# Agent attention with a gated convolution: queries ahead of the first keys, joined score runs, urgent row copies

## Chip, core and metric

One NeuronCore of a Trainium2 chip runs the whole program. The metric is device time in microseconds of one execution, from the median of three timed runs. The engines are TensorE (PE), VectorE (DVE), ScalarE (ACT), GpSimd (POOL) and SyncE (SP), which issues nearly all transfers.

## What is computed

Four batches of 12,800 positions with 128 channels; 49 agents in each batch.

```python
def sm(a, b):
    s = scale * (a @ b.transpose(0, 2, 1))
    s = s - s.max(-1, keepdims=True)
    e = np.exp(s)
    return e / (e.sum(-1, keepdims=True) + 1e-09)
agent_v = sm(agents, k) @ v
x = sm(q, agents) @ agent_v                     # 4 x 12800 x 128
gate_pre = sum(conv_w[k] * x_shifted_by(4 - k) for k in range(5))   # causal, along positions
gate = 1 / (1 + exp(-gate_pre))
out = (gate * (x @ w_val)) @ w_out
```

(The sum over shifts is written out here in short; the reference pads four zeros in front.)

## The kernel before

Positions of a batch are cut into 10 units of 1,280. Units are counted through all batches (0 to 39); pair p is units 2p and 2p + 1. For the output a batch is cut into 25 chunks of 512 (two and a half chunks a unit), counted 0 to 99, the last of them split in two.

The work is written as a list of steps with short names, `x b.u`:

- `k b.u`: scores of a key unit against the agents (TensorE, 16 products in f32, line 391, into one of two PSUM banks `sc`), copied out by ScalarE (line 417), and the maximum of the unit by VectorE (line 426).
- `m b`, in two steps: the maximum over the ten units, turned and spread by TensorE, VectorE and TensorE again, to the bias of the exponents (`kbias`, line 472).
- `v b.u`: exponents of the keys (ScalarE, line 486), turned in 32x32 blocks by VectorE (line 401), and summed against v on TensorE (line 495).
- `f b`, in five steps: the agents' values of a batch are folded with the convolution and the two weight matrices into ready stationary matrices (`stat`, `wo`). Gates of a batch need it.
- `q b.u`: scores of a query unit (TensorE, into a bank `sc`), turned by VectorE (line 401), maximum (VectorE, line 760), difference (GpSimd, line 765), exponent (ScalarE, line 773), sum and reciprocal (VectorE, lines 778, 779, 782), product (VectorE, line 787), and then a high and a low half in f16 in `pt` (ScalarE line 794, GpSimd lines 800 and 808).
- `t b.u`: `pt` is transposed into `x1`, for units 0 to 3 by TensorE (line 863, copied out by ScalarE and VectorE, lines 870 and 875), for all others by a transposing transfer on SP's queue (line 849). Behind that come the row copies (line 898): some rows of `x1` are copied into `x2`, each shifted by 0 to 4 positions, one pair of transfers for each of units 0 to 3, then one pair of transfers for two units at once.
- `g t`, `a t`, `o t`: gate of a chunk (five products from `x1`, line 937, and one from `x2`, line 941, then tanh on ScalarE), values (lines 964 and 968, then VectorE 977, ScalarE 983, GpSimd 988), and projection (lines 1007 to 1009, ScalarE 1021, store from line 1036).

What sets the order: the long string `order` gives the order of the steps, and so that of TensorE's work. The loads of q, k and v stand in the order of their steps, on eleven tiles `ld`, so that a load may run eleven loads ahead. Everything else (the order on VectorE, ScalarE, GpSimd and on SP's queue) is set by `Plan.order`, which runs through all steps with estimated durations and always takes the ready step with the longest chain behind it; `urge` adds to the length of that chain, and by that also to everything that the step needs. Each engine then works strictly through its own row, and SP issues its transfers in its row, each when what it waits for is done.

Of the kernel before, what the change touches and what calls it, by code (L numbers as in the profile page):

```python
# [49 lines left out]
SINGLE = 4  # L50
# [13 lines left out]
SOON = 10.0  # L64
# [6 lines left out]
class Plan:  # L71
# [11 lines left out]
    def add(self, engine, us, fn, reads=(), writes=(), moved=0.0, key=None, urge=0.0):  # L83
        i = len(self.steps)
        need = set()
        for x in reads:
            need |= self.wrote.get(x, set())
        for x in writes:
            need |= self.wrote.get(x, set()) | self.read.get(x, set())
        for x in reads:  # L90
            self.read.setdefault(x, set()).add(i)
        for x in writes:
            self.wrote[x], self.read[x] = {i}, set()
        self.steps.append((engine, us, fn, need, moved, key))
        self.urge.append(urge)
# [84 lines left out]
def tile_agent_attention_gated_conv(  # L180
# [10 lines left out]
    B, C, N = qT.shape  # L191
    A = 49
    NU = N // UNIT
# [19 lines left out]
    m2 = const.tile([P, 2], F32, name="m2")  # L213
# [610 lines left out]
    def row_keys(s, halves):  # L824


        i = s % NX
        return [(x, i, h) for h in halves for x in ("x1", "x1b")] + [("x1h", i)] * (0 in halves)

    def halo(s, read=()):  # L830
        to = x1s[s % NX][:, PAD - HALO : PAD]
        if s * 2 % NU == 0:
            fn = lambda: nc.gpsimd.memset(to, 0.0)
        else:
            fn = lambda: nc.gpsimd.tensor_copy(
                out=to, in_=x1s[(s - 1) % NX][:, PAD + SEG - HALO : PAD + SEG]
            )
        keys = [(x, (s - 1) % NX, 1) for x in ("x1", "x1b")]
        add("pool", 0.19, fn, list(read) + keys, [("x1h", s % NX)])

    def transposes(b, u):
# [3 lines left out]
        if not on_pe(b, u):  # L845
            dst = unit_rows(g)
            add(
                "dma", 1.4,
                lambda: nc.sync.dma_start_transpose(
                    out=dst.rearrange("p (n i) -> p n i", i=P),  # L850
                    in_=pt.rearrange("p n r -> p (n r)"),
                ),
                [(*p_, n) for n in range(3)], [("x1", g // 2 % NX, g % 2)], 2.4,
            )
            shifts(b, u)
            return
# [4 lines left out]
        def matmuls():  # L861
# [14 lines left out]
            [at], [("x1b", g // 2 % NX, g % 2)],  # L876
        )
        shifts(b, u)

    def shifts(b, u):  # L880

        g = b * NU + u
        if g >= SINGLE and g % 2 == 0:
            return
        n = 1 if g < SINGLE else 2
        u0 = u + 1 - n
        s = g // 2
        x2, x1 = x2s[s % 3], x1s[s % NX]
        o = (g + 1 - n) % 2 * UNIT
        src = row_keys(s, range(0, g % 2 + 1))  # L890
        c = PAD - HALO + o
        for r0, r1, first, every, us in X2CUTS:
            first += A
            rows = x1[first : first + 1 + (r1 - r0 - 1) * every : every, c : c + 1]
            view = [rows.ap[0], (1, TAPS), (1, n * UNIT)]
            add(
                "dma", 0.6,
                lambda r0=r0, r1=r1, rows=rows, view=view: nc.sync.dma_start(
                    out=x2[X2B + r0 * TAPS : X2B + r1 * TAPS, o : o + n * UNIT],
                    in_=bass.AP(rows.tensor, rows.offset, view),  # L900
                ),
                src, [("x2", s % 3, o + i * UNIT, r0) for i in range(n)], us * n,
                urge=SOON if g < SINGLE else 0.0,
            )
        if g % 2 and g < SINGLE:
            halo(g // 2 + 1)
# [165 lines left out]
    for b in range(B):  # L1072
        t0 = b * NCH
        for i in range(NU):
            g = b * NU + i + LEAD
# [17 lines left out]
    for t in range(len(chunks) + 2):  # L1093
# [7 lines left out]

    kinds = {"m": "max", "f": "fold"}
    order = (
# [25 lines left out]
    )  # L1129
    first = [(kinds.get(x[0], x[0]), *map(int, x[1:].split("."))) for x in order.split()]  # L1130
    for w in first:
# [70 lines left out]
```

## Time and profile before

| | us |
|---|---|
| timed runs | 422.53, 423.37, 424.21 (median 423.37) |
| the profiled execution | 419.86 |
| its span, from the first to the last instruction | 417.9 |
| TensorE busy | 399.7 (96%) |
| ScalarE, VectorE, GpSimd busy | 307.2, 295.2, 237.4 |

All rows below come from that one profiled execution, with times counted from the start of its span. Busy time of TensorE is modelled from its instructions; successive products overlap, so the distance of their starts tells more than their durations. An instruction's idle time in brackets is that of its engine ahead of it, with the work that ended it.

### The profile page before, as it was taken

Reading aid. Unit: us, or ns where it says so; the run is one execution under the profiler, and the core shown is the slowest. Engines: PE = TensorE matmul, PEld = TensorE weight load, DVE = VectorE, ACT = ScalarE, POOL = GpSimd, SP = SyncE. Lnnn points to the kernel's source line nnn. Section 1 sums busy time; section 2 is a strip of 40 time slices with the busy share of each in tenths; the row PEclk is TensorE's granted clock in tenths of the full one; section 3 lists DMA queues with packets and bytes.
Section 4 is the critical chain, followed back from the end, with each engine's and each line's share of the span. In section 5 each row is a group of like instructions: output and inputs, shape, how many; then the busy total and the mean of one; then the engine's idle time right before and its main releaser. Section 6 shows DMA issues by size and latency. Waiting matters only on the chain.

```text
span 417.9 us, 10098 instructions
## 1 busy us (share of the span) xinstructions
PE 399.7 (96%) x3907; PEld 195.2 (47%) x3907; DVE 295.2 (71%) x570; ACT 307.2 (74%) x524; POOL 237.4 (57%) x303
## 2 busy tenths in 40 slices
PE   4978999999999999999999999999999999999995
PEld 1357334336555443345555543344555544344443
DVE  5866889976885977677796685777757598666231
ACT  6584468778957677678987486778877577788775
POOL 1002458655677566564476555585366577787643
PEclk9989999999999999999999999999999999999999
DMA  8999999999999999999999999999999977663823
GB/s 323 418 417 413 356 361 353 303 338 319 413 334 281 284 321 373 354 264 348 352 399 288 279 320 380 295 350 276 323 350 347 271 204 224 187 173 145 247 107 126
DMA packets 75131, 127.63 MB, mean 305 GB/s; under 512 B 50466, under 2 KB 50850, under 8 KB 75084
## 3 DMA queue, kind: packets, MB, share of 16 engines
q1 hardware_dynamic: 74940, 126.87, 96.3%
q8 instruction: 30, 0.49, 0.5%
q10 hardware_dynamic: 144, 0.13, 0.1%
q14 instruction: 17, 0.14, 0.1%
HBM read 79.25 MB, written 26.21 MB: 252 GB/s over the span
## 4 chain that ended last, share of the span: by engine, by line
PE 78%; DMA 11%; DVE 6%; ACT 1%; issue 1%; SPq 1%; POOL 0%; POOLq 0%; DVEq 0%
PE gate L937 24%; PE sc L391 17%; PE av L495 8%; DMA ld<-vP 6%; PE val L964 5%; PE out L1007 5%; PE gate L941 5%; PE val L968 5%; PE out L1008 5%; PE out L1009 4%; DMA ld<-kT 2%; DMA x<-pt 2%; DMA x<-x 1%; DVE h L977 1%; DVE sT L401 1%
## 5 line engine op out<-in xcount | busy, mean ns | idle before, releaser
L988 POOL TENSOR_TENSOR hl<-h,hh 128x512 f16<-128x512 f32 (+1 forms) x101 | 116.7, 1156 | 97.1 <-ACT hh L983 96.8
L937 PE MATMUL gate<-x,stat 128*128 128x512 f16 (+1 forms) x500 | 124.2, 378 | 0.4 <-ACT th L950 0.3
L977 DVE SCALAR_TENSOR_TENSOR h<-th,val 128x512 f32<-128x512 f32 x100 | 67.8, 678 | 62.1 <-PE out L1008 28.3
L391 PE MATMUL sc<-ld,ag_sb 128*32 128x320 f32 x1280 | 101.4, 447 | 7.3 <-DMA ld<-kT 6.7
L950 ACT ACTIVATE th<-gate,unscale 128x512 f32<-128x512 f32 x100 | 68.3, 683 | 32.7 <-PE gate L941 31.3
L1021 ACT ACTIVATE ob<-out,oscale 128x512 f32<-128x512 f32 x98 | 67.2, 686 | 19.1 <-PE out L1009 16.5
L937 PEld LDWEIGHTS <-stat 128*128 128x128 f16 x505 | 46.1, 97 | 63.3 <-issue 13.1
L983 ACT CAST hh<-h 128x512 f16<-128x512 f32 (+1 forms) x101 | 61.4, 608 | 16.6 <-DVE h L977 16.1
L765 POOL TENSOR_TENSOR qw<-sT,qmx 128x490 f32<-128x490 f32 x40 | 41.3, 1034 | 45.0 <-DVE qmx L760 44.7
L391 PEld LDWEIGHTS sc<-ld,ag_sb 128*32 128x32 f32 x1280 | 36.8, 111 | 58.7 <-issue 25.6
L495 PE MATMUL av<-ld,eT 128*32 128x129 f32 (+1 forms) x1400 | 49.6, 276 | 1.5 <-DVE eT L401 1.2
L495 PEld LDWEIGHTS av<-ld,eT 128*32 128x32 f32 (+1 forms) x1400 | 45.6, 115 | 8.4 <-issue 3.0
L808 POOL TENSOR_TENSOR pt<-qw,pt 128x490 f16<-128x490 f32 x40 | 44.8, 1119 | 1.6 <-ACT pt L794 1.4
L401 DVE STREAM_TRANSPOSE sT<-sc 128x640 f32<-128x640 f32 x40 | 33.5, 837 | 12.9 <-PE sc L391 12.2
L486 ACT ACTIVATE e<-ks,kbias 128x320 f32<-128x320 f32 x80 | 39.2, 553 | 3.5 <-DVE eT L401 2.2
L800 POOL TENSOR_SCALAR pt<-qw 128x240 f16<-128x240 f32 x80 | 27.8, 367 | 22.0 <-DVE qw L787 22.0
L401 DVE STREAM_TRANSPOSE eT<-e 128x640 f32<-128x640 f32 x40 | 33.3, 839 | 9.5 <-ACT e L486 5.3
L941 PE MATMUL gate<-x,stat 128*128 128x512 f16 x100 | 37.8, 378 | 0.5 <-DMA x<-x 0.5
L964 PE MATMUL val<-x,stat 128*128 128x512 f16 x100 | 37.9, 379 | 0.2 <-DVE wo L743 0.2
L968 PE MATMUL val<-x,stat 128*128 128x512 f16 x100 | 37.8, 378 | 0.0
L417 ACT COPY ks<-sc 128x640 f32<-128x640 f32 x40 | 27.6, 690 | 13.4 <-PE sc L391 13.0
L1007 PE MATMUL out<-hh,wo 128*128 128x512 f16 x98 | 37.2, 380 | 0.1
(133 smaller groups left out, 418.9 us busy)
## 6 DMA issues: line engine op xcount, KB each, us to landing
ld<-kT SPq DMA_DIRECT2D x40, 640.0 KB
ld<-qT SPq DMA_DIRECT2D x40, 640.0 KB
ld<-vP SPq DMA_DIRECT2D x39, 645.0 KB
outT<-ob SPq DMA_DIRECT2D x48, 512.0 KB
x<-x SPq DMA_DIRECT2D x18, 300.0 KB
x<-x SPq DMA_DIRECT2D x18, 175.0 KB
outT<-ob SPq DMA_DIRECT2D x3, 256.0 KB
ld<-vP SPq DMA_DIRECT2D x2, 322.5 KB
```

Of the source, the lines that this page charges most:

```text
L391: nc.tensor.matmul(out=out[g * BLK : (g + 1) * BLK, j, 0:GT], lhsT=ag_sb[:, b, j * BLK : (j + 1) * BLK], rhs=src[:, g * GT : (g + 1) * GT] ...
L401: nc.vector.transpose(out=out.rearrange("p n (j i) -> p j n i", j=2), in_=in_.rearrange("p j (n i) -> p j n i", i=BLK),)
L495: nc.tensor.matmul(out=av[o + j : o + j + cols, 0 : C + 1], lhsT=et[:, n, j : j + cols], rhs=vt[:, n, :], start=(u == 0 and n < 2), stop=( ...
L937: nc.tensor.matmul(out=pg, lhsT=stat[:, k, :], rhs=x1[:, c : c + w], start=(k == 0), stop=False,)
L941: nc.tensor.matmul(out=pg, lhsT=stat[:, TAPS + 1, :], rhs=x2[:, o2 : o2 + w], start=False, stop=True,)
L950: lambda: nc.scalar.activation(out=th, in_=pg, func=AF.Tanh, scale=unscale[:, 0:1]),
L964: nc.tensor.matmul(out=pv, lhsT=stat[:, TAPS, :], rhs=x1s[(b * NCH + n0 // CH) // 5 % NX][:, PAD + o2 : PAD + o2 + w], start=True, stop=False,
L968: nc.tensor.matmul(out=pv, lhsT=stat[:, TAPS + 2, :], rhs=x2[:, o2 : o2 + w], start=False, stop=True,)
L977: lambda: nc.vector.scalar_tensor_tensor(out=h, in0=th, scalar=1.0, in1=pv, op0=ALU.add, op1=ALU.mult),
L983: "act", 0.16 + 0.42 * scale, lambda: nc.scalar.copy(out=hh, in_=h),
L988: lambda: nc.gpsimd.tensor_tensor(out=hl, in0=h, in1=hh, op=ALU.subtract),
L1021: lambda: nc.scalar.activation(out=ob[:, o : o + w], in_=po, func=AF.Copy, scale=oscale),
```

## The change

Three edits. The steps q0.0, q0.1 and q0.2 stand ahead of the ten key units of batch 0 instead of behind them, with their transposes t0.0, t0.1 and t0.2 among the keys and the key maximum. In the later part of the order runs of score and sum steps that were parted by a gate, values or projection step are put next to each other, at thirteen places. And `urge` for row copies, which was given for units 0 to 3 (`SINGLE` is 4), is given for units 4 and 5 too, and for the last pair of units of batches 0, 1 and 2.

```diff
-                urge=SOON if g < SINGLE else 0.0,
+                urge=SOON if g < SINGLE + 2 or u == NU - 1 and b < B - 1 else 0.0,
...
-        "k0.0 k0.1 k0.2 k0.3 k0.4 k0.5 k0.6 k0.7 k0.8 k0.9 m0 m0 q0.0 v0.0 v0.1 v0.2 v0.3 v0.4 "
-        "v0.5 v0.6 v0.7 v0.8 v0.9 f0 t0.0 f0 q0.1 k1.0 f0 k1.1 f0 q0.2 g0 k1.2 f0 t0.1 a0 q0.3 "
+        "q0.0 q0.1 q0.2 k0.0 k0.1 k0.2 t0.0 k0.3 k0.4 k0.5 k0.6 k0.7 k0.8 k0.9 t0.1 m0 t0.2 m0 "
+        "v0.0 v0.1 v0.2 v0.3 v0.4 v0.5 v0.6 v0.7 v0.8 v0.9 f0 k1.0 f0 k1.1 k1.2 f0 q0.3 f0 g0 "
...
```

What this makes of the engines' rows at three places (numbers behind names are those of the buffers; `x8` stands for eight equal products, two passes each).

VectorE in the opening, before: from the middle of the weights' unpacking (`ob`, lines 311 to 342) over the first key maxima (`kmx`).

```order
L326 CAST ob1_121<-ob1_121 128x261
L426 TENSOR_REDUCE kmx0_73<-ks_72 128x2
L311 TENSOR_SCALAR ob1_121<-ob1_121 128x261
L426 TENSOR_REDUCE kmx0_73<-ks_72 128x2
L328 SCALAR_TENSOR_TENSOR ob1_121<-ob1_121 128x261
L332 TENSOR_TENSOR ob1_121<-ob1_121 128x261
L426 TENSOR_REDUCE kmx0_73<-ks_72 128x2
L311 TENSOR_SCALAR ob1_121<-ob0_120 128x261
L426 TENSOR_REDUCE kmx0_73<-ks_72 128x2
```

The same engine in the opening now, from the third query's scores to the first key maximum and one half of t0.0's copy.

```order
L401 STREAM_TRANSPOSE sT0_85<-sc1_135 128x2x10x32
L778 TENSOR_REDUCE qsm0_93<-qw0_89 128x10
L779 SCALAR_TENSOR_TENSOR qsm0_93<-qsm0_93,tiny_146 128x10
L782 RECIPROCAL qr0_95<-qsm0_93 128x10
L787 TENSOR_TENSOR qw0_89<-qw0_89,qr0_95 128x490
L760 TENSOR_REDUCE qmx0_87<-sT0_85 128x10
L778 TENSOR_REDUCE qsm1_94<-qw1_90 128x10
L779 SCALAR_TENSOR_TENSOR qsm1_94<-qsm1_94,tiny_146 128x10
L782 RECIPROCAL qr1_96<-qsm1_94 128x10
L787 TENSOR_TENSOR qw1_90<-qw1_90,qr1_96 128x490
L426 TENSOR_REDUCE kmx0_73<-ks_72 128x2
L875 COPY x1_0_101<-sc1_135 128x640
```

The query chains stand where the weights' unpacking stood, ahead of all ten key maxima; most of the unpacking now follows the seventh maximum.

TensorE at the projection of chunk 19 (o19), before: k2.0 and k2.1, the projection, k2.2 and q1.4.

```order
L391 MATMUL sc1_135<-ld10_71,ag_sb_145 32x320 x8
L391 MATMUL sc0_134<-ld0_61,ag_sb_145 32x320 x8
L1007 LDWEIGHTS wo160_128
L1007 MATMUL out_138<-hh1_115,wo160_128 128x512
L1008 LDWEIGHTS wo160_128
L1008 MATMUL out_138<-hh1_115,wo160_128 128x512
L1009 LDWEIGHTS wo160_128
L1009 MATMUL out_138<-hl1_118,wo160_128 128x512
L391 MATMUL sc1_135<-ld1_62,ag_sb_145 32x320 x8
L391 MATMUL sc0_134<-ld2_63,ag_sb_145 32x320 x8
```

The same engine and place now.

```order
L1007 LDWEIGHTS wo160_128
L1007 MATMUL out_138<-hh1_115,wo160_128 128x512
L1008 LDWEIGHTS wo160_128
L1008 MATMUL out_138<-hh1_115,wo160_128 128x512
L1009 LDWEIGHTS wo160_128
L1009 MATMUL out_138<-hl1_118,wo160_128 128x512
L391 MATMUL sc1_135<-ld10_71,ag_sb_145 32x320 x8
L391 MATMUL sc0_134<-ld0_61,ag_sb_145 32x320 x8
L391 MATMUL sc1_135<-ld1_62,ag_sb_145 32x320 x8
L391 MATMUL sc0_134<-ld2_63,ag_sb_145 32x320 x8
```

The projection moved ahead of the four score tiles, which now follow each other on the two banks `sc0` and `sc1`.

SP's queue at units 8 and 9 (pair 4, the last of batch 0), before: their two transposing transfers and the row copies into `x2`, with the loads and stores around them.

```order
L384 DMA ld10_71<-kT 128x1280
L384 DMA ld0_61<-kT 128x1280
L1036 DMA outT<-ob1_121 128x1024
L384 DMA ld1_62<-kT 128x1280
L849 DMA_TRANSPOSE x1_0_101<-pt0_97 128x10x128
L384 DMA ld2_63<-qT 128x1280
L849 DMA_TRANSPOSE x1_0_101<-pt1_98 128x10x128
L1036 DMA outT<-ob2_122 128x1024
L384 DMA ld3_64<-kT 128x1280
L384 DMA ld4_65<-qT 128x1280
L898 DMA x21_106<-x1_0_101 60x1x2560
L898 DMA x21_106<-x1_0_101 35x1x2560
```

The same queue and pair now.

```order
L384 DMA ld7_68<-qT 128x1280
L849 DMA_TRANSPOSE x1_0_101<-pt0_97 128x10x128
L849 DMA_TRANSPOSE x1_0_101<-pt1_98 128x10x128
L384 DMA ld8_69<-vP 128x1290
L384 DMA ld9_70<-vP 128x1290
L1036 DMA outT<-ob1_121 128x1024
L898 DMA x21_106<-x1_0_101 60x1x2560
L898 DMA x21_106<-x1_0_101 35x1x2560
L384 DMA ld10_71<-kT 128x1280
L384 DMA ld0_61<-kT 128x1280
```

Both transposes moved ahead of two v tiles, three key tiles and a store, and the row copies ahead of five loads and a store.

## Rows read from the trace of the kernel before

**Rows 1.** The page: TensorE's busy share in tenths, in 40 slices of the span.
```profile
PE   4978999999999999999999999999999999999995
```
**Rows 2.** Waits of TensorE: us in total, times, longest.
```profile
PE sc L391 <- DMA ld<-kT: 6.7, 4, 5.8
```
**Rows 3.** Chain that ended last: start, us, what.
```profile
24.21 12.61 DMA ld<-vP
```
**Rows 4.** A stretch: us, busy of PE, PEld, DVE, ACT, POOL, clock, DMA, GB/s.
```profile
25.80:29.40 3.60, 3.56 (x38) 3.56 (x40) 2.54 (x3) 3.10 (x8) 0.00 (x0) 0.59 1.03 423
```
**Rows 5.** Timeline of the opening: start, us, engine, line, operation, count, idle before.
```profile
8.27 0.69 ACT L417 COPY ks<-sc 128x640 f32<-128x640 f32 x1 [1.26 <-PE sc L391]
...
23.63 0.16 DVE L472 TENSOR_SCALAR kbias<-gate 128x2 f32<-128x2 f32 x1 [0.31 <-PE gate L464]
...
25.84 9.35 PE L495 MATMUL av<-ld,eT 128*64 128x129 f32 x140 [1.03 <-DVE eT L401]
...
36.96 2.42 PE L495 MATMUL av<-ld,eT 128*64 128x129 f32 x40 [0.29 <-DMA ld<-vP]
...
48.22 1.25 PE L937 MATMUL gate<-x,stat 128*128 128x512 f16 x5
...
66.04 1.24 PE L937 MATMUL gate<-x,stat 128*128 128x512 f16 x5
```
**Rows 6.** VectorE's operations of queries and key maxima: shortest, median, longest in ns.
```profile
L401 DVE STREAM_TRANSPOSE sT<-sc x40: 786/844/851, 30.6 to 375.6; 128x640 f32<-128x640 f32 x40
...
L778 DVE TENSOR_REDUCE qsm<-qw x40: 619/657/666, 35.2 to 380.5; 128x10 f32<-128x490 f32 x40
...
L760 DVE TENSOR_REDUCE qmx<-sT x40: 614/656/665, 32.0 to 376.4; 128x10 f32<-128x490 f32 x40
...
L782 DVE RECIPROCAL qr<-qsm x40: 216/216/218, 36.1 to 381.4; 128x10 f32<-128x10 f32 x40
...
L779 DVE SCALAR_TENSOR_TENSOR qsm<-qsm,tiny x40: 170/171/1050, 35.9 to 381.2; 128x10 f32<-128x10 f32 x40
...
L787 DVE TENSOR_TENSOR qw<-qw,qr x40: 622/664/1505, 36.9 to 381.7; 128x490 f32<-128x490 f32 x40
...
L426 DVE TENSOR_REDUCE kmx<-ks x39: 748/814/821, 9.0 to 283.9; 128x2 f32<-128x640 f32 x39
```
**Rows 7.** Timeline of GpSimd and VectorE at 217.7.
```profile
217.67 1.10 POOL L808 TENSOR_TENSOR pt<-qw,pt 128x490 f16<-128x490 f32 x1
217.74 1.05 DVE L779 SCALAR_TENSOR_TENSOR qsm<-qsm,tiny 128x10 f32<-128x10 f32 x1
```
**Rows 8.** Timeline of TensorE: two joined score tiles, and a lone one.
```profile
71.68 0.38 PE L964 MATMUL val<-x,stat 128*128 128x512 f16 x1
71.90 0.38 PE L968 MATMUL val<-x,stat 128*128 128x512 f16 x1
...
74.50 0.39 PE L1007 MATMUL out<-hh,wo 128*128 128x512 f16 x1
...
79.93 0.38 PE L941 MATMUL gate<-x,stat 128*128 128x512 f16 x1
...
81.46 0.39 PE L964 MATMUL val<-x,stat 128*128 128x512 f16 x1
```
**Rows 9.** Timeline of TensorE and ScalarE: score tiles and the copy of one.
```profile
55.88 2.36 PE L391 MATMUL sc<-ld,ag_sb 128*32 128x320 f32 x32 [0.58 <-DVE sT L401]
...
158.51 1.28 PE L391 MATMUL sc<-ld,ag_sb 128*32 128x320 f32 x16
...
159.86 0.69 ACT L417 COPY ks<-sc 128x640 f32<-128x640 f32 x1 [0.83 <-PE sc L391]
```
**Rows 10.** Waits and timeline at row copies; SP's transposing transfers: shortest, median, longest ns.
```profile
PEld L941 <- DMA x<-x: 1.5, 3, 1.0
...
233.86 0.38 PE L941 MATMUL gate<-x,stat 128*128 128x512 f16 x1 [0.51 <-DMA x<-x]
...
L849 SPq DMA_TRANSPOSE x<-pt x36: 1352/2679/7929, 73.4 to 388.9; - x36
```

45 rows, old and new, of the table order are left out of this document.

## The prediction

> **What bounds the kernel now.** I read the page first, then the waits, then the timeline. On the page TensorE's row of slices stands at 9 from the fifth slice to the last but one [rows 1]. So there are two stages: an opening of some 60 us in which TensorE has gaps, and a dense stage behind it in which it goes from one product to the next. In the opening its longest wait is for the first key tile [rows 2]; the chain of waits then runs over the transfers of v, the last full tile of which lands at 24.21 + 12.61 = 36.8 us [rows 3]. The last tile, as large (660 KB, 1.57 us at the 423 GB/s of [rows 4]), comes at about 38.4, and the products of the agent sums end at 36.96 + 2.42 = 39.4 [rows 5]. Then the fold of batch 0 runs as a chain over all engines, the first gate product starts at 48.22, and the fourth (chunk 3) at 66.04 [rows 5]; from there TensorE is dense. Whatever changes before 66.04 counts as the time at which chunk 3 starts, and whatever comes later as TensorE time or as a new wait.
>
> **The opening, part by part.** Ahead of chunk 3 both orders hold the same work: q0.0 to q0.5, k1.0 to k1.5, t0.0 to t0.3, three chunks of gates and values, one projection. Only its place changes.
>
> *Transfers.* Two more query tiles (655 KB, 1.57 us each) and the row copies of unit 0 (95 rows of 2,560 bytes, 0.6 us at the rate of [rows 4], at most as much as a tile, 1.6) now stand ahead of the last v tile: it lands at 38.4 + 3.1 + 0.6 to 1.6 = 42.1 to 43.1. This alone would put the end of the agent sums at about 44.
>
> *VectorE.* The exponents of the keys need all ten key maxima. Before, nothing but the weights' unpacking stands beside those, and the bias is ready at 23.63 [rows 5]. Now three query chains stand ahead: each 0.84 + 0.65 + 0.65 + 0.17 + 0.22 + 0.66 = 3.2 us of VectorE [rows 6], 9.6 in all. The first scores leave TensorE at about 8.3 (the first key copy in [rows 5]). From there VectorE owes 9.6 for queries, 10 x 0.81 = 8.1 for maxima [rows 6], and about 3 for small things by my estimate (one half of t0.0's copy, four unpacking steps, the reduction itself); with 1 us of waits for the second and third scores, which TensorE gives at half pace there, the maxima are complete at 30. The step from there to the bias takes 1.5 us before; t0.2 now stands on TensorE between its two halves, 0.7 more by my estimate for ten transposes of 128x128. That gives about 31.7 instead of 23.63, eight us later.
>
> One row decides whether this holds. At 217.74 VectorE's tiny L779, whose median is 0.17 us, takes 1.05 and ends with the GpSimd operation that started at 217.67 [rows 7]; L787 goes from 0.66 to 1.5 in its worst case [rows 6]. GpSimd is idle there before [rows 4], and now runs three query chains there. I put half a collision of 0.9 us into the 31.7; none gives 31.2, and a full one at every L779 and L787 of the three queries (six times 0.85) gives 36.3. The Trainium skill (SBUF — State Buffer, section "SBUF: two separate sides") says that VectorE with two SBUF inputs and a GpSimd operation that reads SBUF take a shared port pair as an exclusive lock for the whole instruction. The trace agrees where the two meet; by that rule every meeting costs what is left of the GpSimd operation, which speaks against queries in the opening.
>
> *From the bias to chunk 3.* Before, the first agent product starts 25.84 - 23.63 = 2.2 us behind the bias, and the first seven tiles take 9.35 [rows 5], the first of them at a mean granted clock of 0.59 [rows 4] after a pause of TensorE. The pause is there again, so I take the same 9.35, and 1.1 for each of the last three (40 products in 2.42 are at most 1.2 a tile). That ends at 31.7 + 2.2 + 9.35 + 3.3 = 46.5, behind the 44 of the transfers: VectorE has taken the place of the loads. The fold's chain before is 48.22 - 39.4 = 8.8 to the first gate product, with one query's scores (1.2) too many at its end; now 7.6, plus 0.2 for key maxima ahead of a weights' copy: first gate at 54.3. From there to chunk 3 TensorE has three gates of six product steps, three values of two and a projection of three, at 0.215 a step ([rows 8] round it to 0.22): 3 x 1.29 + 3 x 0.43 + 0.65 = 5.8, five score tiles in three runs (2 x 2.38 + 1.31 = 6.1, from [rows 8]), and by my estimate 0.6 for t0.3 and 0.3 for the last fold step: 12.8, where before it took 17.8 with four more steps (k1.2, q0.3, t0.1, t0.2) and waits in it. Chunk 3 starts at 67.1 against 66.04: **+1.0** (bounds: -1.3 if the transfers set it, +5.6 with all six collisions).
>
> **The dense stage.** *Joined runs.* Between gate products a lone score tile takes 81.46 - 79.93 = 1.53 from product start to product start; two together take 74.50 - 71.90 = 2.60 [rows 8]. Two lone ones hold one ordinary product step (71.90 - 71.68 = 0.22) more, so a join is worth 2 x 1.53 - 2.60 - 0.22 = 0.24. The dense stage is TensorE's, nothing hides it: 13 x 0.24 = **-3.1**.
>
> *Banks.* Scores alternate between two PSUM banks, so the third tile of a run waits until the first is drained. In [rows 9] this once cost 0.58, with a query drained late by VectorE. A key tile that starts at 158.51 is drained by 159.86 + 0.69 = 160.55, 2.04 behind its start, and two tiles take 2 x 1.08: just in time. Nine third or fourth tiles appear in the new order; I take 0.1 in sum (0 to 2.6, half of 0.58 at each of nine).
>
> *Urgent copies.* Three times the weights of a gate's last product wait for row copies, 1.5 us in all, mostly beside products that still run; at 233.86, in the first chunk of batch 1's last pair, the product itself comes 0.51 late [rows 10]. The change hurries that pair, its like in batches 0 and 2, and units 4 and 5. The order shows both transposes and the row copies of such a pair ahead of loads and stores that they stood behind, and on GpSimd the work that feeds them earlier by one to three chunks. **-0.5** (0 to -0.5); the loads that it passes are hidden by the eleven tiles of read-ahead, and in TensorE's list of waits the first keys are the only load that it waited for in earnest [rows 2].
>
> *The pairs that are not hurried.* A transpose stands up to 7.9 us on SP's queue [rows 10], and pairs 5, 10, 15 and 16 (pair p is units 2p and 2p + 1) have their transposes or copies behind one more store, that is two chunks or 4.8 us. TensorE waited for none of them before, so they have spare time of unknown size: **+0.3** (0 to 3.5).
>
> Sum: +1.0 - 3.1 + 0.1 - 0.5 + 0.3 = **-2.2**; the profiled execution has 419.86 in all with a span of 417.9, 3.5 under the median of 423.37. The difference is applied to the median: **421.2**.
>
> **The rivals.**
> *The transfers set the opening:* VectorE's chain is shorter than I count, the agent sums end near 44, chunk 3 starts 1.3 earlier. For it: transfers run without a gap to 37 before. -1.3 - 3.1 + 0 - 0.5 + 0 = -4.9: 418.5.
> *VectorE and GpSimd collide throughout (slower):* the bias comes at 36.3, and everything in the opening moves by 4.6 more: +5.6 - 3.1 + 0.1 - 0.5 + 0.3 = +2.4: 425.8. It loses against before from a bias later than 34. The page named above (SBUF — State Buffer, of the Trainium skill) would have it so wherever the two run at once. Against it: in the dense stage most L779 keep their 0.17.
> *Joins eaten by banks:* 2.6 instead of 0.1, 423.7; against it stands the drain that is just in time.
> *Unhurried pairs fall late:* 3.5 instead of 0.3, 424.4.
> *The urgency does not reach the copies*, since SP waits for the same GpSimd work as before: 0.5 is lost, 421.7; the orders of SP and GpSimd speak against it, and it lies in the forecast's own spread.
>
> **How the numbers follow.** Forecast 0.50, own range 419.9 to 422.5; transfers 0.15; collisions 0.15; banks 0.10; unhurried pairs 0.10. About 0.5%, 2.1 us, is what a measurement of this kernel can tell from no change, so the forecast lies at the edge: just over half of it (0.28) and the transfers' case give 0.43 faster; the rest of it, the banks and most of the unhurried pairs 0.40; collisions and a little else 0.17 slower. The range of 8 in 10 goes from 418.8, which cuts off part of the transfers' case, to 424.7, which leaves out most of the collisions.
>
> **What would show it.** The bias (L472 of batch 0) at 31 to 32, the last agent product of batch 0 ending at 46 to 47, the first gate at about 54 and chunk 3 at 66 to 68; long L779 or L787 before 24 us would show collisions. TensorE's score groups x48 and x64 with waits under 0.2 before the third tile; no wait at the first chunk of the last pair in batch 1; from chunk 3 to the end about 3.2 us less than the 351.9 of before. The prediction is wrong if the bias comes before 30 or behind 34, or if new waits for row copies over 1 us appear.

## The result: slower, and where the time went

Beside each other on one chip the kernel before took 422.95 us and the changed one 426.65 (medians of four executions each); the ratio is **1.0103, 95% interval 1.0060 to 1.0146**. The profiled execution of the changed kernel has a span of 423.4 against 417.9, so 5.5 us are to be found. (The ratio leaves out executions that stand out as disturbed, here one of 432.93 us, and the medians do not; where the two disagree, below too, the ratio counts.)

The opening came out close to its forecast. VectorE in the changed kernel, columns start, duration, engine, line, operation, tiles:

```profile
13.74 0.17 DVE L779 SCALAR_TENSOR_TENSOR qsm<-qsm,tiny 128x10 f32<-128x10 f32 x1
...
16.05 0.68 DVE L779 SCALAR_TENSOR_TENSOR qsm<-qsm,tiny 128x10 f32<-128x10 f32 x1
...
17.01 1.19 DVE L787 TENSOR_TENSOR qw<-qw,qr 128x490 f32<-128x490 f32 x1
...
20.65 0.51 DVE L779 SCALAR_TENSOR_TENSOR qsm<-qsm,tiny 128x10 f32<-128x10 f32 x1
...
30.62 0.15 DVE L472 TENSOR_SCALAR kbias<-gate 128x2 f32<-128x2 f32 x1
```

And TensorE at the agent sums, at the first gate and at the gate of chunk 3:

```profile
32.87 14.16 PE L495 MATMUL av<-ld,eT 128*64 128x129 f32 x200 [2.42 <-DVE eT L401]
...
53.86 1.24 PE L937 MATMUL gate<-x,stat 128*128 128x512 f16 x5
...
66.75 1.24 PE L937 MATMUL gate<-x,stat 128*128 128x512 f16 x5
```

The bias is ready at 30.8, the agent sums end at 32.87 + 14.16 = 47.0, the first gate starts at 53.86, and chunk 3 at 66.75, 0.7 behind the 66.04 of [rows 5]. From chunk 3 to the end it is 423.4 - 66.75 = 356.7 where it was 351.9: 4.8 us are lost in the dense stage, where 3.2 were to be won.

TensorE's products that wait there, in the changed kernel; the bracket is the idle time ahead and what ended it:

```profile
255.71 0.39 PE L941 MATMUL gate<-x,stat 128*128 128x512 f16 x1 [1.40 <-DMA x<-x]
...
292.78 0.39 PE L941 MATMUL gate<-x,stat 128*128 128x512 f16 x1 [1.63 <-DMA x<-x]
...
334.20 0.38 PE L941 MATMUL gate<-x,stat 128*128 128x512 f16 x1 [1.60 <-DMA x<-x]
```

These are the first chunks of pairs 10, 12 and 14. From the start of one product to the next they are 1.57, 1.79 and 1.76 us late, 5.1 in all. The wait of [rows 10], 0.68 when counted in the same way, is gone: the hurried pair 9 now has 2.0 us to spare. The chain of waits runs over these copies (start, duration):

```profile
249.91 5.75 DMA x<-x
...
285.45 7.28 DMA x<-x
...
326.79 7.37 DMA x<-x
```

Two smaller losses. Where a joined run has a third score tile, that tile waits for a bank; TensorE and ScalarE in the changed kernel at k2.4, k2.5 and q1.6:

```profile
160.25 2.36 PE L391 MATMUL sc<-ld,ag_sb 128*32 128x320 f32 x32
162.92 1.28 PE L391 MATMUL sc<-ld,ag_sb 128*32 128x320 f32 x16 [0.32 <-ACT ks L417]
```

```profile
162.19 0.69 ACT L417 COPY ks<-sc 128x640 f32<-128x640 f32 x1
```

ScalarE drains the first key tile only at 162.19 + 0.69 = 162.88, and the third tile starts at 162.92. By product starts five runs lose 0.52, 0.48, 0.18, 0.16 and 0.10, **1.4** in all. And a score run that was moved away sometimes had covered another wait. TensorE at chunk 14, changed kernel:

```profile
109.13 0.38 PE L968 MATMUL val<-x,stat 128*128 128x512 f16 x1
109.98 1.24 PE L937 MATMUL gate<-x,stat 128*128 128x512 f16 x5 [0.47 <-ACT th L950]
```

Here the gate waits until ScalarE has drained the one gate bank (tanh, line 950). In the kernel before v1.4 stands in this place, and the gate behind it does not wait:

```profile
108.74 0.38 PE L968 MATMUL val<-x,stat 128*128 128x512 f16 x1
109.05 1.31 PE L495 MATMUL av<-ld,eT 128*32 128x129 f32 x40
110.29 1.04 PE L937 MATMUL gate<-x,stat 128*128 128x512 f16 x4
```

Ten such gaps of 0.1 to 0.6 us, by product starts, come to 3.1, where before had 0.5 (gaps that both kernels have are left out): **+2.6**.

The joins save more than I counted: at two of the thirteen places (k2.4 k2.5 q1.6 and k3.1 k3.2 k3.3 q2.5) three runs become one, so there are fifteen runs fewer, at 0.235 each 3.5 us. The expectations below still go by 13 x 0.235 = 3.0. The account: +0.7 (opening), -3.5 (joins), +1.4 (banks), +4.4 (copies, 5.1 - 0.7), +2.6 (small waits) = +5.6, where 5.5 are measured.

### The profile page after: what moved, and what is told of

It is laid out like the page before. It is cut to its first block, busy times and chain, and to the rows that moved or that the text cites. A ratio compares the mean times of both kernels' runs of the same rounds, so it can differ in the third digit from the quotient of the medians.

```text
span 423.4 us, 10092 instructions
## 1 busy us (share of the span) xinstructions
PE 398.9 (94%) x3907; PEld 198.4 (47%) x3907; DVE 298.7 (71%) x570; ACT 306.4 (72%) x524; POOL 236.4 (56%) x303
## 2 busy tenths in 40 slices
DMA packets 75131, 127.63 MB, mean 301 GB/s; under 512 B 50466, under 2 KB 50850, under 8 KB 75084
## 4 chain that ended last, share of the span: by engine, by line
PE 55%; DVE 16%; POOL 10%; DMA 9%; ACT 4%; issue 4%; SPq 0%; POOLq 0%; DVEq 0%; ACTq 0%
PE gate L937 15%; PE sc L391 11%; PE av L495 10%; DMA x<-x 6%; POOL hl L988 4%; PE val L964 3%; PE gate L941 3%; PE out L1007 3%; PE val L968 3%; PE out L1008 3%; PE out L1009 3%; DVE h L977 3%; POOL pt L808 2%; DVE kmx L426 2%; POOL qw L765 2%
## 5 line engine op out<-in xcount | busy, mean ns | idle before, releaser
L391 PE MATMUL sc<-ld,ag_sb 128*32 128x320 f32 x1280 | 99.6, 446 | 7.9 <-DMA ld<-qT 6.0
L495 PEld LDWEIGHTS av<-ld,eT 128*32 128x32 f32 (+1 forms) x1400 | 47.4, 117 | 7.3 <-DVE eT L401 2.5
L941 PE MATMUL gate<-x,stat 128*128 128x512 f16 x100 | 37.8, 378 | 4.6 <-DMA x<-x 4.6
```

Source lines behind the costliest of these rows:

```text
L391: nc.tensor.matmul(out=out[g * BLK : (g + 1) * BLK, j, 0:GT], lhsT=ag_sb[:, b, j * BLK : (j + 1) * BLK], rhs=src[:, g * GT : (g + 1) * GT] ...
L495: nc.tensor.matmul(out=av[o + j : o + j + cols, 0 : C + 1], lhsT=et[:, n, j : j + cols], rhs=vt[:, n, :], start=(u == 0 and n < 2), stop=( ...
L941: nc.tensor.matmul(out=pg, lhsT=stat[:, TAPS + 1, :], rhs=x2[:, o2 : o2 + w], start=False, stop=True,)
```

## The experiments

Each difference in us below is the ratio applied to 421, about the median of before beside these runs. "Spare time" of a pair is how long its two row copies have landed, by the trace, before its first chunk's L941 would start without them; negative is a wait.

### One part at a time

The urgency edit alone:

```diff
-                urge=SOON if g < SINGLE else 0.0,
+                urge=SOON if g < SINGLE + 2 or u == NU - 1 and b < B - 1 else 0.0,
```

> The kernel before with the urgency edit alone (order of before). In the trace of after, TensorE waits 1.56, 1.79 and 1.76 us for row copies at the first chunks of pairs 10, 12 and 14, and no longer 0.68 at pair 9. Theory A (urgency pushes the unhurried pair 10 behind the fold of batch 2 on GpSimd, and the delay is passed on to pairs 11 to 14): the same three waits are here, pair 9 has none, +3 to +4.5 us, 426 to 427.5. Theory B (the joined runs make the copies late): no wait at pairs 10, 12, 14, pair 9 gains its 0.7, 422 to 422.5. Theory C (only the two together use up the spare time): one wait at most, 422.5 to 424.

Ratio 1.0017 (0.9991 to 1.0044), no difference. One small new wait at pair 15 (0.54 by starts). Theory A falls: urgency on its own makes pairs 10, 12 and 14 wait for nothing. It does take spare time from pairs 10 and 12 (table below).

The new opening alone (the steps up to chunk 3 from the change, the rest from before):

```diff
-        "k0.0 k0.1 k0.2 k0.3 k0.4 k0.5 k0.6 k0.7 k0.8 k0.9 m0 m0 q0.0 v0.0 v0.1 v0.2 v0.3 v0.4 "
+        "q0.0 q0.1 q0.2 k0.0 k0.1 k0.2 t0.0 k0.3 k0.4 k0.5 k0.6 k0.7 k0.8 k0.9 t0.1 m0 t0.2 m0 "
...
```

> The kernel before with the new opening alone (three queries ahead of the keys, up to chunk 3), the old order behind it and no new urgency. All theories: bias near 30.6, first gate near 53.9, chunk 3 at 66.7 to 67.0 instead of 66.04, and the dense stage as in before (351.9 from chunk 3 to the end), so +0.7: 423.7. If the later order of the engines' rows depends on the opening, copy waits appear here and it is above 425.

Ratio **1.0153** (1.0114 to 1.0191): 6.4 us, though chunk 3 starts at 66.24, 0.2 behind before. The expectation had named copy waits as a possibility. TensorE's waits in this kernel, at the first chunks of pairs 2, 4 and 9:

```profile
95.22 0.39 PE L941 MATMUL gate<-x,stat 128*128 128x512 f16 x1 [1.23 <-DMA x<-x]
...
138.22 0.39 PE L941 MATMUL gate<-x,stat 128*128 128x512 f16 x1 [1.21 <-DMA x<-x]
...
238.97 0.38 PE L941 MATMUL gate<-x,stat 128*128 128x512 f16 x1 [2.50 <-DMA x<-x]
```

By starts 1.39, 1.37 and 2.67. (The 1.05 that the next expectations add is no wait but products at half clock behind the last one; see the end.) From chunk 10 on the order of rows on VectorE, ScalarE and GpSimd is that of before. On SP it is that of before again from the row copies of pair 8 on (199 us in before); up to there single loads and stores stand in other places, and the transposes of pair 4 stand ahead of one more load. The copies of pairs 4 and 9 are issued 2.9 and 5.0 us later, while TensorE itself reaches their chunks 1.7 and 3.1 later. For pair 9, around which all rows stand as before, the order nearby is not what makes it late. That the order ahead of it is not enough either shows only further below, where the same rows with fewer bytes have no wait.

The thirteen joined runs alone, of which one stands here:

```diff
-        g26 a26 t1.5 k2.4 o24 q1.6 g27 k2.5 a27 o25
+        g26 a26 t1.5 o24 k2.4 k2.5 q1.6 g27 a27 o25
```

> The kernel before with the thirteen joined runs alone. The joins save 13 x 0.235 = 3.0 us of TensorE steps. In after, the five joined runs with a third score tile waited 0.52, 0.48, 0.18, 0.16 and 0.10 for a bank, 1.4 in all, and small waits for other engines came to 2.6. Theory A: no copy waits beyond those of before; with the bank waits alone 421.4, with the small waits too 424. Theory B: the waits at pairs 10, 12 and 14 are here, 5 us, 426 to 428. Theory C: one wait at most, 421.5 to 424.5.

Ratio 1.0051 (1.0021 to 1.0082), 2.1 us. One wait of 3.03 by starts, at pair 2. Theory B falls by this: pairs 10, 12 and 14 do not wait. The opening and the joined runs together, without the new urgency (the change with the first diff of this section undone):

> The changed kernel without its urgency edit (new opening and joined runs). Theory A (urgency makes the copies late): the waits at pairs 10, 12 and 14 are gone, about 5 us less than after, and the 0.7 at pair 9 is back: 421.5 to 423. Theory B (the joins do it): the three waits stay, 426 to 427.5. Theory C: one or two stay, 423 to 425.

Ratio 1.0190 (1.0158 to 1.0222), 8 us: worse than after, with 5.18 by starts at pair 9 and 0.71 at pair 14:

```profile
239.33 0.60 PE L941 MATMUL gate<-x,stat 128*128 128x512 f16 x1 [5.01 <-DMA x<-x]
```

So the urgency helps: it takes some 3.7 us off. The spare times show why (us; pairs 2, 4, 9 and 14 were just in time before):

```
pair             2     4     9    10    12    14
before         0.0   0.2  -0.6   7.4   3.0   0.2
urgency only   2.6   5.8   2.2   0.8   1.9   0.8
opening only  -1.3  -1.3  -2.6   8.0   3.9   1.1
joins only    -3.0   1.8   4.0  12.1   6.4   3.6
after          2.3   7.3   2.0  -1.5  -1.7  -1.7
```

### Two parts, and more urgency

The opening with the urgency, and the joined runs with the urgency:

> New opening and new urgency, old runs behind chunk 3. The opening alone measured +6.4 with waits of 1.39, 1.37, 2.67 and 1.05 us for the row copies of pairs 2, 4 and 9, whose spare time in the kernel before is 0.0, 0.2 and none. Theory D (the copies of those pairs have no spare time; the opening moves them by 2 to 5 us; urgency buys them back and takes the time from the pairs behind them): no wait at pairs 2, 4 and 9, so 4 to 5 us under the opening alone, but up to 2 us of waits at pairs 10 to 14: 422 to 424.5. Theory A (urgency itself makes pairs 10, 12 and 14 late, 5 us): 426 or more.

> Joined runs and new urgency on the old opening. The joined runs alone measured 423.1 with one wait of 3.03 us at pair 2. Theory D: urgency takes that wait away, and without the new opening the pairs from 10 on keep enough spare time: 419.5 to 421, at or under before. Theory E (joined runs and urgency together make pairs 10, 12 and 14 late, as in after): waits of 3 to 5 us there, 423.5 to 426.

Ratios 1.0062 (1.0021 to 1.0103) and 1.0102 (1.0025 to 1.0179). The first is nearly as theory D has it: 3.8 us less than the opening alone, with 1.7 at pair 10 and 0.6 at pair 15, but 0.8 is left at pair 9. The second is not: the joined runs win nothing by the urgency and rather lose (the intervals overlap). That is in the range of theory E, but where this run waits is left open here. Then urgency for every unit, and the change on the old opening without the five joined runs that waited for a bank:

```diff
-                urge=SOON if g < SINGLE + 2 or u == NU - 1 and b < B - 1 else 0.0,
+                urge=SOON,
```

> The changed kernel with the urgency for every unit and pair. Theory F (the harm is that unhurried pairs, 10 and 12, are pushed behind hurried ones and behind loads): the waits at pairs 10 and 12 go, 3.4 us less than after, 421.5 to 423.5. Theory G (urgency only passes time from one pair to the next, SP and GpSimd have no more of it): waits of 3 us or more stay at some pairs, 424.5 to 428.

> As joined runs and urgency on the old opening, without the five joined runs in which a third score tile waited for a bank (k2.4 k2.5 q1.6; k2.6 k2.7 q1.7; q1.8 k2.8 k2.9; k3.6 q2.7 k3.7; q2.8 k3.8 k3.9). If those waits are the banks', 1.4 us of them goes and five joins of 0.235 are given back, 1.2: equal to the run with all thirteen joins within 0.5, and no wait of over 0.1 before a third tile. If the copies depend on where the queries stand, waits at pairs 12 and 14 change too and it differs by 1 to 2 us.

Ratios 1.0207 (1.0141 to 1.0273) and 1.0108 (1.0041 to 1.0174). With all pairs hurried the waits at pairs 10 and 12 shrink to 0.6 and 0.45 and pair 14's grows to 2.15, and late in the kernel other work waits instead (a projection 1.3, a values step 1.0, a gate 0.9). That is theory G, the time is passed on, though 429.7 by the ratio is slower than it said. The other kernel has no bank waits left, as expected, and is as fast as the run with all joins within 0.5; but it waits 0.9 at pair 9, 2.1 at pair 10 and 1.5 at pair 12, so its time told nothing of the banks.

### What makes the copies late

One resource had been full all along. The stretch from 66 to 300 us in the kernel before; the last three columns are the granted clock, the DMA engines' share and GB/s:

```profile
66.00:300.00 234.00, 233.31 (x2437) 111.73 (x2434) 177.06 (x328) 178.84 (x313) 142.91 (x176) 1.00 1.09 327
```

And in the changed kernel:

```profile
66.00:300.00 234.00, 229.26 (x2349) 111.06 (x2347) 175.75 (x327) 176.35 (x307) 141.16 (x176) 1.00 1.08 321
```

By the share the sixteen DMA engines are busy without a gap in both (the profile adds up packets that overlap, hence over 1). So bytes were taken away with every instruction, the order and the number of packets (75,131) kept, in four kernels; of 127.6 MB 104.7 are left:

```diff
-                out=outT[b, :, n0 + w - n : n0 + w], in_=ob[:, lo : lo + n]
+                out=outT[b, :, n0 + w - n : n0 + w - n + n // 8], in_=ob[:, lo : lo + n // 8]
```

> The kernel before, storing only the first eighth of each block of the output (the rest of the output is left out): the instructions of all engines and their order are the same, 22 of 127 MB fewer are moved. In before the DMA engines are busy without a gap from 66 to 300 us (share 1.08 to 1.10). Theory H (the row copies come late because they stand in the DMA engines behind other bytes): copies land 2 us or more sooner after their issue, the wait of 0.68 at pair 9 goes, 419.5 to 420.5, and spare time appears at pairs 2, 4, 9 and 14. Theory I (they are late because of SP's order, behind transposes that wait for GpSimd): same waits and same spare times within 0.7, 420.5 to 421.5.

> The changed kernel, storing only the first eighth of each block of the output. Theory H: the waits of 1.57, 1.79 and 1.76 at pairs 10, 12 and 14 go; left are +0.7 of the opening, -3.0 of the joins, +1.4 of the banks and up to +2.6 of small waits: from 1 us under to 1.7 over before with the same stores. Theory I: waits of 3 us or more stay, 4 us over it.

> The opening alone, storing only the first eighth of each block. With full stores it was 6.4 over before, nearly all of it waits at pairs 2, 4 and 9 and a stretch at half clock behind the last. Theory H: these go, 0 to 1 us over before with the same stores. Theory I: 4 us or more over it.

> The joined runs alone, storing only the first eighth of each block. With full stores 2.1 over before, with a wait of 3.03 at pair 2. Theory H: that wait goes; the joins' 3.0 less bank waits of 1.4 and small waits of 0 to 2.6 is left: from 1.6 under to 1 over before with the same stores. Theory I: 2 us over it.

Medians of twelve executions each: **419.15, 418.81, 419.14 and 419.66**, every execution between 417.9 and 420.4, while the kernel before beside them went from 419.1 to 426.2. The four kernels that were up to 6.4 us apart are now within 0.9. After has no wait for a copy left (spare at pairs 10, 12 and 14: 10.6, 10.8 and 12.8); only the joined runs alone keep one, 1.06 at pair 2. This is theory H with a miss: copies do not land sooner behind their issue (pair 9 of before 227.0 to 233.8, now 220.1 to 226.6); they are issued 6.8 us sooner. SP's row says why. Before with all stores:

```profile
210.64 7.93 SPq L849 DMA_TRANSPOSE x<-pt  x1
```

Before with an eighth of the stores:

```profile
210.72 1.84 SPq L849 DMA_TRANSPOSE x<-pt  x1
```

GpSimd's rows at this place are the same to a tenth, in before and in before with an eighth:

```profile
213.04 0.68 POOL L800 TENSOR_SCALAR pt<-qw 128x240 f16<-128x240 f32 x2
```

```profile
213.12 0.69 POOL L800 TENSOR_SCALAR pt<-qw 128x240 f16<-128x240 f32 x2
```

The same transposing transfer, issued at the same time behind the same GpSimd work, holds SP for 7.93 us or for 1.84, and everything behind it on SP, the row copies among it, waits. The profile's table of waits puts these stretches down to GpSimd's `hl` and `pt`; that is not what releases them. The share itself does not tell the two apart. The changed kernel with an eighth of the stores:

```profile
66.00:300.00 234.00, 232.28 (x2441) 113.57 (x2439) 178.63 (x333) 178.50 (x312) 142.85 (x179) 1.00 1.00 288
```

It still reads 1.00, and no copy waits. What the mean hides is how often the engines run short: counted from the packets of the traces, fewer than sixteen are in flight for 4% of this stretch in before and 5% in the changed kernel, but for 21% and 22% with an eighth of the stores. Two more runs part the bytes from SP's rows: half of each block stored (`n // 2` in the line above), and all of it stored, but issued from ScalarE:

```diff
-            lambda: nc.sync.dma_start(
+            lambda: nc.scalar.dma_start(
```

> The changed kernel, storing only the first half of each block of the output: 12.6 of 127 MB fewer, the same rows on SP. With all stores 1.0% over before, with an eighth 0.8% under it. If the bytes in the DMA engines make the copies late: waits for copies under 1 us in all instead of 5.1, 419 to 421; the transposes' median on SP between 1.55 (an eighth) and 3.23 us (all). If something else of the stores does it: 423 or more.

> The changed kernel with every store of the output issued from ScalarE's queue instead of SP's; the same bytes. If the bytes in the DMA engines make the copies late: waits for copies of 3 us or more stay, 424 to 428, and the transposes still stand on SP for a median of 2.5 us or more. If the rows of the stores on SP's in-order queue do it: the copies are issued some us earlier, waits under 1.5 us in all, 420 to 422. ScalarE, 72% busy, can lose by it what the issues cost there (0.4 to 0.5 us for each of 53): where the copies do not wait and TensorE waits for ScalarE instead, the time says nothing and the copies' spare times decide.

Half: 418.78, no copy waits, and the share is between the two:

```profile
66.00:300.00 234.00, 232.26 (x2441) 113.55 (x2439) 178.65 (x333) 178.47 (x312) 142.71 (x179) 1.00 1.05 312
```

From ScalarE: ratio 1.064, 449 us, with a copy wait of 6.4 at pair 2 and long ones for ScalarE; the time says nothing. Nor do the spare times, which were to decide then: at pairs 10, 12 and 14 they are 2.8, 7.9 and 7.5, but the copies are issued 17 to 20 us later than in after, and TensorE reaches these chunks 23 to 28 us later. What is left to compare is how long the transposes hold SP. The transposes on SP's queue (count, then min/median/max in ns, first and last start) in after:

```profile
L849 SPq DMA_TRANSPOSE x<-pt x36: 1305/3230/8625, 73.1 to 394.4; - x36
```

in after with half of the stores, and with an eighth:

```profile
L849 SPq DMA_TRANSPOSE x<-pt x36: 1306/2262/6330, 72.5 to 388.5; - x36
```

```profile
L849 SPq DMA_TRANSPOSE x<-pt x36: 1302/1553/4358, 72.4 to 388.5; - x36
```

and in after with its stores issued from ScalarE:

```profile
L849 SPq DMA_TRANSPOSE x<-pt x36: 1278/3555/8288, 71.6 to 418.3; - x36
```

Medians of 3.23, 2.26 and 1.55 us: the hold follows the bytes. And it is 3.56 without the stores' rows on SP: it does not follow those. The Trainium skill (DMA: Bandwidth & Descriptors, section "Issuing engines are not separate DMA queues") says that transfers started by any engine run on the same sixteen DMA engines, and that another issuer saves only the time that the issue takes. This agrees: the share stays at 1.08 there. Its remark that this time is usually small does not hold for the transposes here: 3.23 us in the median in after, where the issue of a row copy takes 0.81. Whether it is the bytes as such or that they are written to HBM was not parted, and by what a full set of DMA engines holds up the issue of a transpose no run shows.

### Why the joins bring nothing even then

With fewer stores the joins should have shown their saving less the 1.4 for banks; they showed +0.5 alone and -0.3 in the change. Seven that lose little in the trace of after, and the six that lose most, each alone on the kernel before, as in the diff above for joined runs:

> The kernel before (old opening, old urgency) with seven of the thirteen joins (k1.8 k1.9; q1.8 k2.8 k2.9; q2.2 v2.6 v2.7; k3.6 q2.7 k3.7; q2.8 k3.8 k3.9; q2.9 v3.0 v3.1; q3.2 v3.5 v3.6 v3.7), storing only the first eighth of each block of the output. If the loss sits where the trace of after shows it: 7 x 0.235 = 1.65 saved, 0.45 lost to banks, so 1.2 under the 419.15 of before with the same stores, 417.8 to 418.2. If it is spread over all joins: 418.9 to 419.4.

> As that, with the other six joins instead (q1.1 v1.4 v1.5; k2.0 k2.1 k2.2 q1.4; k2.4 k2.5 q1.6; k2.6 k2.7 q1.7; k3.1 k3.2 k3.3 q2.5; q3.7 q3.8). If the loss sits there: 6 x 0.235 = 1.4 saved, 1.0 lost to banks and 1.9 to 2.4 to small waits, 1.5 to 2 over before with the same stores, 420.6 to 421.2. If it is spread: 419 to 419.5.

418.52 and 419.66 beside 419.15: -0.6 and +0.5, the signs as expected, the sizes half or a third of it. By time alone this is not clear of noise (ratios to before with all stores 0.9908, 0.9874 to 0.9943, and 0.9949, 0.9923 to 0.9975, beside 0.9929, 0.9898 to 0.9960, for before with an eighth). The traces are clearer. From the first gate product of chunk 3 to the last product of the kernel, all with an eighth of the stores, in us against before:

```
                      joins alone   change   seven   six
runs fewer                     15       15       7     8
saved, at 0.235              -3.5     -3.5    -1.6  -1.9
waits for a bank             +1.5     +1.4    +0.2  +1.1
small waits                  +1.5     +2.5    +0.4  +1.5
waits for a copy             +1.1      0.0    +0.6   0.0
sum                          +0.6     +0.4    -0.4  +0.7
measured                     +0.6     +0.3    -0.4  +0.7
```

So the saving is there, and waits for banks and small waits eat it. Most of the loss sits in the six. In the seven's trace two new waits (0.57 at pair 2, 0.53 at a transpose in the fold) stand against the gain; in the six's, the gate of chunk 14 no longer waits and the next values step does (0.47). The small waits also hang on how the planner lays the other engines' rows, and by what rule a join opens one stays open. The opening, of the same steps in all but the change, moves by more than these differences: chunk 3 starts at 66.17 in the trace of before and at 67.61 in that of the seven. With all stores the seven:

> The seven joins with all stores, old opening and old urgency. If the copies of pairs 2, 4, 9 and 14 keep their spare time of 0 to 0.2, the part of the 1.2 us that is won ahead of them comes back as waits: 420 to 421.5, the same as before or up to 1 under it. If the saturated DMA engines push them back as in the other runs: 422 to 424.

Ratio 1.0060 (1.0020 to 1.0100), with 3.17 at pair 2, as the second reading has it. k1.8 and k1.9 joined, 10 us ahead of it, seems to be enough; that one join was not run alone. No version under the kernel before came out of this.

## Why the prediction was wrong

Its own sign of being wrong appeared: new waits for row copies over 1 us. Term by term, forecast and then measured: opening +1.0 and +0.7, joins -3.1 and -3.5, banks 0.1 and 1.4, the wait at pair 9 -0.5 and -0.7, the pairs that have to give 0.3 and 5.1, small waits nothing and 2.6.

- *Opening: right, in part by luck.* Bias 30.8 (forecast 31 to 32), agent sums 47.0 (46 to 47), first gate 53.86 (about 54), chunk 3 +0.7 (+1.0). VectorE set it and not the transfers: the 200 agent products run without a wait for v. Three of the six L779 and L787 were long, by 0.51, 0.34 and 0.53 over [rows 6], 1.4 us where I had put 0.45. A GpSimd operation ran beside each of these three and beside none of the other three; that agrees with the lock of the Trainium skill (SBUF — State Buffer, "SBUF: two separate sides") as far as these six go. The rest was counted 1.9 us too long, which made up for it. And the addends of the bias (30 + 1.5 + 0.7) give 32.2, not the 31.7 that the prediction goes on with.
- *Joins: price right, outcome wrong.* Every run still costs 0.45 beyond its tiles, whatever its length, so 0.235 a run holds, and there were fifteen runs fewer and not thirteen. The banks took 1.4 instead of 0.1: the drain "just in time" of [rows 9] was one key tile with ScalarE idle; with ScalarE behind its own row it is 0.5 late. And the 2.6 of small waits had no term at all: I counted what a lone run costs and not what it covers.
- *Urgent copies: right in place.* The wait of [rows 10] is gone and pairs 2, 4 and 9 have spare time. That the hurry could cost other pairs something had no term ("0 to -0.5").
- *Pairs not hurried: this step failed.* "TensorE waited for none of them before, so they have spare time of unknown size" was priced at 0.3, at most 3.5; new waits for copies came to 5.1. The spare time could have been read: 0.0, 0.2 and 0.2 us at pairs 2, 4 and 14, none at 9, and at 9 and 2 the opening alone and the joins alone do wait. But the smallest spare time was not the whole of it. Pairs 10 and 12 had 7.4 and 3.0; with the urgency alone 0.8 and 1.9 are left of it, and with the opening added pair 10 waits. I looked for the loss at pairs 5, 10, 15 and 16; of these only 10 came, while 12 and the hurried 14 came too.
- *What stood behind it:* I took the 7.9 us of a transpose in [rows 10] as given, looked to GpSimd for what SP waits on, and used the DMA engines only for the opening. They are busy to 300 us, and the hold of the transposes follows the bytes: that is what makes the copies just in time or late. Why the time lost comes out at one pair and not at another is read from the spare times above and not explained by them. The rival that I had for this ("unhurried pairs fall late", 0.10) was the right one, and too small; "joins eaten by banks" was half right as well.

## What to carry to other kernels

Before a saving on the busiest engine is counted, read the DMA share of the same stage. A share at 1 or over is a warning and no more: here the saving came back as waits for copies at 1.08, and none waited at 1.00 and 1.05. Read the spare time of every transfer that is hidden now, not only of those that show a wait, and read it again for each part of a change: hurrying one transfer took the time from others that had had 3 to 7 us. To find out whether a late transfer is due to bytes or to its order, take bytes away and leave all instructions in place. And count what a piece of work covers before it is moved, not only what it costs.

## What was not expected of the hardware

- A transposing transfer holds SP's in-order queue for 1.3 to 8.6 us in the changed kernel, the longer the more bytes are moved beside it (medians 3.23, 2.26 and 1.55 us with all, half and an eighth of the stores), and the plain copies behind it wait with it.
- Most of the scatter of the kernel before (419.1 to 426.2) goes with the bytes: 418.8 to 419.75 with an eighth of the stores.
- Behind some waits TensorE's granted clock fell from its full level, 2.4 GHz, to 1.2 GHz for some us. Behind the wait at 238.97 in the run with the opening alone (2.50 us idle) it was 0.58 of full in the mean from 239 to 243 us, six product steps at 0.43 instead of 0.22 us and some others longer in the same way:

```profile
239.00:243.00 4.00, 4.00 (x14) 2.08 (x15) 2.07 (x7) 1.30 (x2) 1.35 (x2) 0.58 1.15 320
```

Behind the 5.01 us of the opening with the joins, at the same pair, it was 0.50:

```profile
239.00:243.00 4.00, 3.67 (x11) 1.97 (x12) 1.95 (x6) 1.30 (x2) 0.67 (x1) 0.50 1.16 299
```

Behind 2.87 us in the run with the joins alone it stayed at full speed:

```profile
96.64 0.39 PE L941 MATMUL gate<-x,stat 128*128 128x512 f16 x1 [2.87 <-DMA x<-x]
```

```profile
96.60:98.00 1.40, 1.36 (x17) 0.64 (x21) 0.00 (x0) 0.87 (x2) 0.00 (x0) 1.00 0.89 180
98.00:101.00 3.00, 3.00 (x87) 2.42 (x80) 2.27 (x3) 2.50 (x6) 2.19 (x2) 1.00 1.26 240
```

And behind a shorter one, 2.0 us at pair 14 with every pair hurried, it fell to 0.54 (332.3 to 336 us). So the length of the one wait does not decide it; what does these runs do not show. Of the 6.4 us of the opening alone this is some 1.6.
